# Attention and two expert layers on one core: a second PSUM bank for the sums of products with v, one bank fewer for the products of the maxima, no pause between heads

## The chip, the cores and the metric

The kernel runs on one core of one Trainium2 chip. The metric is the device time of one execution in microseconds; the time of a kernel is the median of its runs. Five engines work side by side on a core: TensorE (PE, with its weight loads shown as PEld), VectorE (DVE), ScalarE (ACT), GpSimd (POOL) and SyncE (SP), which here issues loads and stores (DMA). Each works through its own instructions in order and waits on semaphores for what others produce. TensorE writes its results into PSUM, a memory in banks, and VectorE and ScalarE read them there.

## What is computed

An attention in which each query sees only the keys of its own cluster, then a mixture of experts with one expert for each token, then a dense layer. Cut to what matters:

```python
# B, H, S, D = 2, 8, 768, 64; 16 clusters
q_assign = argmax(einsum('bhsd,hcd->bhsc', q_n, c_n)); k_assign likewise
mask = q_assign[:, :, :, None] == k_assign[:, :, None, :]
scores = where(mask, (q @ k.T) / sqrt(D), -1e9)
attn = exp(scores - scores.max(-1)); attn /= attn.sum(-1) + 1e-9
x = (attn @ v)                       # -> 1536 tokens x 512
e = argmax(x @ w_gate + modality_bias[modality_id])       # 8 experts
x = gate[e] * (relu(x @ w1[e]) @ w2[e])                   # 512 -> 1024 -> 512
h = x @ w_in                                              # 512 -> 2048
out = (h * tanh(softplus(h))) @ w_out                     # 2048 -> 512
```

## The kernel before

There are 16 heads (2 batches of 8), numbered i, and each head has six blocks of 128 keys, numbered kt. `attention()` is a generator that walks over n = 6 i + kt. For each n it does, in program order:

- `st_step`: four matmuls (L391) that give the transposed scores of one block of keys against all 768 queries, in two tiles of one PSUM bank each (`s` from pool `ps_s`, or `eps` from `ps_e`), and two exponentials on ScalarE (L393). ScalarE then rounds the result to f16 (`eh`, L400) and GpSimd forms the remainder (`el`, a subtraction in L114); for kt 2 and 5 it is used in f32 as it is (`ef`).
- `smax`: the row maxima of a head one to two ahead. Matmuls of the masked products (L350 with 512 columns; L355 twice 256 columns) write a tile `x` of pool `ps_x`, one bank each, nine for a head. VectorE reduces each tile to maxima (L351, L356) and, after the six blocks, to `mx` (L363). ScalarE makes `m16` of it (L366), six transposes (`mrow_b`, L373) write one more tile `x`, and ScalarE copies it into the operand of the next head (L378). So the scores of a head wait for the maxima of that head.
- `av_step`: the sums of products with v, three blocks behind (LAG = 3). For each block 18 matmuls (L427, L428, L429 with `eh` and `el`) or 6 in f32 (L425) add into the head's tile `av` of pool `ps_a`, which takes one bank for the whole head. `fin` reads it when the head is done: VectorE forms r from the sums (L440, L441) and xt (L442), ScalarE and GpSimd write the two halves of x.

`assign` finds the clusters of a head three ahead: 24 small matmuls (L273), a chain on VectorE (L286, L287, L289, L290, L292, L299) and GpSimd, a copy on ScalarE, and four DMAs that write the result into the head's operand `QK` (L303). `stack` loads the operand of a head three ahead with four DMAs (L258 to L261). At the start of head 1, `gate_consts` loads the constants of the gate with three DMAs, and twelve slots later VectorE prepares them (L683 to L693).

Pieces like `fin`, `assign` and `gate_consts` lie in a list `side`, from which `slot()` takes one or two at each of three places in a step. `avq` holds the blocks whose sums are due, and `av_next` takes one or two of them at two places in a step. It also holds a pause: when the head before is finished it sets `gap[0] = GAP`, and at the first block of the next head it returns so many times without work, so that the sums of the new head, which need the one bank of `ps_a`, are issued a step later.

The order in which instructions then stand on PE, DVE, ACT and POOL is not the program order: a scheduler lays all instructions out on a modelled time line, in which each PSUM bank is free again after its last reader, and fixes the order of each engine from it. SyncE keeps the program order. So another number of banks moves instructions on several engines all through attention.

After batch 0 is gated (`gate`), expert matmuls (L1027, `moe1`) and the conversion of w_in (`convs`, L1047 to L1055) are mixed into the heads of batch 1. When attention is over its pools are closed, four banks go to the last part (L1027 into `h`, L1183 into `o`), and the rest of the experts runs beside it.

Eight banks are held by four pools while attention runs: `ps_e` 2 (tag `e`), `ps_s` 2, `ps_x` 3, `ps_a` 1.

Of the kernel before, what the change touches and what calls it, by code (L numbers as in the profile page):

```python
# [16 lines left out]
PSUM = bass.MemoryType.PSUM  # L17
# [7 lines left out]
def clustered_attention_moe_kernel(  # L25
# [32 lines left out]
    LOWD = ()  # L58
    LOWE = ()
    PREG = 12  # L60
    GAP = 1
    AVL = 1
    ASK = 2
    CV1 = 20
# [29 lines left out]
    att = ExitStack()  # L94
# [5 lines left out]
    dp = ctx.enter_context(tc.tile_pool(name="dp", bufs=1, space=DRAM))  # L100
    ps_e = ctx.enter_context(tc.tile_pool(name="ps_e", bufs=2, space=PSUM))
    ps_s = att.enter_context(tc.tile_pool(name="ps_s", bufs=2, space=PSUM, side="right"))
    ps_x = att.enter_context(tc.tile_pool(name="ps_x", bufs=3, space=PSUM, side="right"))
    ps_a = att.enter_context(tc.tile_pool(name="ps_a", bufs=1, space=PSUM, side="right"))
    ap = att.enter_context(tc.tile_pool(name="ap", bufs=1, side="right"))
    a2 = att.enter_context(tc.tile_pool(name="a2", bufs=2, side="right"))
    a3 = att.enter_context(tc.tile_pool(name="a3", bufs=3, side="right"))
# [386 lines left out]
    def attention():  # L494
# [41 lines left out]
        def av_next():  # L536

            k = 1 + (len(avq) > AVL)
            while avq and k:
# [9 lines left out]
                if j == 1 and kt == T - 1:  # L549
                    gap[0] = GAP  # L550
                    if i % H == H - 1 and FAST:
# [840 lines left out]
```

## Time and profile before

| | us |
|---|---|
| three runs, median | 678.7 (677.6 to 678.86) |
| the profiled execution | 680.72 |
| its span in the profile | 679.0 |
| PE busy | 620.5 (91%) |
| ACT busy | 454.6 (67%) |
| DVE busy | 378.3 (56%) |
| POOL busy | 255.4 (38%) |

The table gives averages over a span with different parts. Attention reaches to about 312 us; behind it stand the experts and the dense layers. A matmul's row ends with a modelled drain, and matmuls overlap, so rows of PE that follow each other closely start more often than their lengths suggest, and a PE that is "busy" is not at its peak. An engine's wait is told in the views by the instruction that ended it ("<- DVE xt L442": the wait ended when VectorE's L442 had written xt). PEclk is the clock that TensorE was granted, as a share of its full speed.

### The profile page before, as it was taken

The page shows a single profiled execution, that of the slowest core. Times are in us where ns is not written, and L with a number is a line of the kernel's source. Part 1 is how long each engine was busy: PE and PEld are TensorE (multiplying, and loading weights), DVE is VectorE, ACT ScalarE, POOL GpSimd, SP SyncE. Part 2 cuts the span into 40 slices and gives each one's busy share as a digit, 9 for nine tenths or more (in the row PEclk, how much of TensorE's full clock was granted, in tenths as well). Part 3 has the DMA queues.
Part 4 walks back from the last instruction along what each step waited for, and adds up shares of the span by engine and source line. Part 5 has one row for each costly group of instructions (what it writes and reads, how often), then busy time and mean ns, then how long its engine had stood idle before and what let it go on. Part 6 is the DMA issues. An engine that isn't in the chain of part 4 may idle for free. (4 is left out here: it accounts for less than half of the span.)

```text
span 679.0 us, 13674 instructions
## 1 busy us (share of the span) xinstructions
PE 620.5 (91%) x5474; PEld 424.5 (63%) x5475; DVE 378.3 (56%) x747; ACT 454.6 (67%) x704; POOL 255.4 (38%) x226
## 2 busy tenths in 40 slices
PE   1798989989788998998999899999999999999995
PEld 1476768858466765665766567566666667666442
DVE  5776667687879899989658899622311101101000
ACT  4686787977787777655888686665655576767300
POOL 5464875886865344320521221111311222223111
PEclk9797999999899999999999999999999999999998
DMA  7542343412872353473455555211000000000000
GB/s 230 150 85 54 89 140 104 110 42 61 257 221 75 107 155 94 141 206 120 143 152 204 156 156 178 70 49 46 32 1 1 16 17 0 32 1 16 17 32 35
DMA packets 56742, 64.42 MB, mean 95 GB/s; under 512 B 10080, under 2 KB 46944, under 8 KB 56672
## 3 DMA queue, kind: packets, MB, share of 16 engines
q1 hardware_dynamic: 42064, 48.74, 25.3%
q10 hardware_dynamic: 12688, 8.42, 4.1%
q0 software_dynamic: 1920, 6.32, 2.6%
q8 instruction: 45, 0.74, 0.5%
q14 instruction: 25, 0.20, 0.1%
HBM read 46.23 MB, written 6.32 MB: 77 GB/s over the span
## 5 line engine op out<-in xcount | busy, mean ns | idle before, releaser
L114 POOL TENSOR_TENSOR el<-e,eh 128x768 f16<-128x768 f32 x64 | 108.0, 1691 | 84.9 <-ACT eh L400 52.1
L1027 PE MATMUL h<-x,win 128*128 128x256 f16 x1152 | 131.8, 273 | 0.2 <-POOL x L1014 0.2
L1027 PEld LDWEIGHTS <-win 128*128 128x128 f16 x1152 | 112.6, 98 | 19.0 <-issue 0.4
L1027 PEld LDWEIGHTS <-w 128*128 128x128 f16 x768 | 74.4, 98 | 66.8 <-issue 11.1
L1132 DVE SCALAR_TENSOR_TENSOR s<-s,h 128x512 f32<-128x512 f32 x48 | 30.8, 684 | 148.9 <-ACT s L1128 148.9
L1183 PE MATMUL o<-wout,xb 128*128 128x512 f16 x432 | 95.9, 379 | 0.0
L114 POOL TENSOR_TENSOR xb<-s,xb 128x1024 f16<-128x1024 f32 x18 | 40.2, 2231 | 134.0 <-ACT xb L1135 134.0
L391 PE MATMUL s<-QK 128*128 128x384 f16 x320 | 78.6, 335 | 5.8 <-issue 2.1
L1027 PE MATMUL eps<-xw,w 128*128 128x416 f16 x384 | 72.8, 339 | 8.2 <-DVE hT L989 2.9
L1027 PE MATMUL eps<-hT,w 128*128 128x416 f16 x384 | 71.8, 339 | 1.6 <-DVE hT L989 1.6
L351 DVE TENSOR_REDUCE mxh<-x 128x1 f32<-128x512 f32 x96 | 64.7, 681 | 14.6 <-PE x L350 14.2
L1183 PEld LDWEIGHTS <-xb 128*128 128x128 f16 x432 | 42.2, 98 | 48.3
L393 ACT ACTIVATE e<-s 128x384 f32<-128x384 f32 x112 | 52.5, 489 | 23.1 <-PE s L391 19.1
L400 ACT ACTIVATE eh<-e 128x768 f16<-128x768 f32 x64 | 54.1, 847 | 0.8
L425 PE MATMUL av<-vst,ef 128*128 128x65 f32 x384 | 51.1, 276 | 0.0
L425 PEld LDWEIGHTS av<-vst,ef 128*128 128x128 f32 x384 | 49.8, 196 | 1.9
L427 PE MATMUL av<-vst,eh 128*128 128x65 f16 x384 | 46.0, 195 | 5.2 <-DVE xt L442 4.7
L391 PEld LDWEIGHTS <-QK 128*128 128x128 f16 x384 | 34.6, 103 | 22.1 <-issue 10.0
L1126 ACT ACTIVATE s<-h,cst 128x512 f32<-128x512 f32 x48 | 32.9, 685 | 21.7 <-PE h L1027 21.5
L428 PE MATMUL av<-vst,eh 128*128 128x64 f16 x384 | 46.2, 196 | 0.0
L350 PE MATMUL x<-QK 128*128 128x512 f16 x96 | 37.9, 404 | 8.6 <-DMA QK<-oT 5.1
L942 DVE SCALAR_TENSOR_TENSOR w<-wf,w 128x1024 f16<-128x1024 f32 x32 | 43.4, 1357 | 3.9 <-ACT w L938 3.9
(244 smaller groups left out, 1100.9 us busy)
## 6 DMA issues: line engine op xcount, KB each, us to landing
wf<-in_moe_w_dram ACTq DMA_DIRECT2D x16, 512.0 KB
raw<-in_moe_w_in_dram SPq DMA_DIRECT2D x16, 512.0 KB
raw<-in_moe_w_out_dram SPq DMA_DIRECT2D x16, 512.0 KB
wf<-in_moe_w_dram SPq DMA_DIRECT2D x16, 512.0 KB
QK<-hl SPq DMA_DIRECT2D x32, 192.0 KB
xs<-dr SPq DMA_DIRECT2D x12, 258.0 KB
t<-in_k_dram SPq DMA_DIRECT2D x8, 384.0 KB
t<-in_q_dram SPq DMA_DIRECT2D x8, 384.0 KB
```

The source lines that it names most:

```text
L114: nc.gpsimd.tensor_tensor(out=out_, in0=in0, in1=in1, op=ALU.subtract)
L350: nc.tensor.matmul(sp, lhsT=st[:, QA, t * P:(t + 1) * P], rhs=st[:, KA, 0:512], start=True, stop=True)
L351: nc.vector.reduce_max(out=mx_t[i][:, t, 0:1], in_=sp, axis=AX.X)
L391: nc.tensor.matmul(sps[hf][:, 0:HS], lhsT=st[:, KA + a, kt * P:(kt + 1) * P], rhs=st[:, QA + a, hf * HS:(hf + 1) * HS], start=(a == 0), st ...
L393: nc.scalar.activation(out=e32[:, hf * HS:(hf + 1) * HS], in_=sps[hf][:, 0:HS], func=AF.Exp, scale=1.0 / float(D) ** 0.5)
L400: nc.scalar.activation(out=eh, in_=e32, func=AF.Copy)
L425: nc.tensor.matmul(av[:, t, :], lhsT=e32[:, cols], rhs=vs[:, h, :], start=(kt == 0 and t == 0), stop=(kt == T - 1), skip_group_check=True)
L427: nc.tensor.matmul(av[:, t, :], lhsT=eh[:, cols], rhs=vs[:, h, 0:NV], start=(kt == 0 and t == 0), stop=False, skip_group_check=True)
L428: nc.tensor.matmul(av[:, t, 0:D], lhsT=eh[:, cols], rhs=vs[:, h, NV:], start=False, stop=False, skip_group_check=True)
L942: nc.vector.scalar_tensor_tensor(out=hl_[:, 1], in0=f, scalar=32.0, in1=hl_[:, 0], op0=ALU.mult, op1=ALU.subtract)
L1027: nc.tensor.matmul(out_, lhsT=wc[:, a, kk, ms], rhs=mv[:, c, kk, :], start=(i == 0), stop=(i == n - 1))
L1183: nc.tensor.matmul(pts[t], lhsT=gsl[q % 2][f // FB][:, f % FB, a, t * P:(t + 1) * P], rhs=wout[:, c, f, :], start=(f == 0 and i_ == 0), st ...
```

## The change

Three numbers change. `ps_x`, the pool of the tiles of maxima, gets two banks instead of three; `ps_a`, the pool of the sums, gets two instead of one, so that the sums of one head can begin while `fin` of the head before still reads its own; GAP, the pause of `av_next` at a new head, is 0. The banks in use remain eight. No instruction is added or removed.

```diff
@@ -58,7 +58,7 @@
     LOWD = ()
     LOWE = ()
     PREG = 12
-    GAP = 1
+    GAP = 0
     AVL = 1
     ASK = 2
     CV1 = 20
@@ -100,8 +100,8 @@
     dp = ctx.enter_context(tc.tile_pool(name="dp", bufs=1, space=DRAM))
     ps_e = ctx.enter_context(tc.tile_pool(name="ps_e", bufs=2, space=PSUM))
     ps_s = att.enter_context(tc.tile_pool(name="ps_s", bufs=2, space=PSUM, side="right"))
-    ps_x = att.enter_context(tc.tile_pool(name="ps_x", bufs=3, space=PSUM, side="right"))
-    ps_a = att.enter_context(tc.tile_pool(name="ps_a", bufs=1, space=PSUM, side="right"))
+    ps_x = att.enter_context(tc.tile_pool(name="ps_x", bufs=2, space=PSUM, side="right"))
+    ps_a = att.enter_context(tc.tile_pool(name="ps_a", bufs=2, space=PSUM, side="right"))
     ap = att.enter_context(tc.tile_pool(name="ap", bufs=1, side="right"))
     a2 = att.enter_context(tc.tile_pool(name="a2", bufs=2, side="right"))
     a3 = att.enter_context(tc.tile_pool(name="a3", bufs=3, side="right"))
```

What the change does to the order shows best at three places. In these rows a number behind a name tells tiles of one name apart.

The first place is the turn from head 0 to head 1 on PE. `av_541` are the sums of head 0, `av_806` (before) and `av_803` (after) those of head 1; x_748 belongs to the maxima of head 2, x_844 to those of head 3; s_836, eps_835 and s_766 are scores of head 1. Before:

```order
L350 MATMUL x_844<-QK3_120 128x512
L391 LDWEIGHTS QK1_118
L391 MATMUL s_836<-QK1_118 128x384
L391 LDWEIGHTS QK1_118
L391 MATMUL s_836<-QK1_118 128x384
L427 LDWEIGHTS eh_650
L427 MATMUL av_806<-vst_293,eh_650 128x65
L428 LDWEIGHTS eh_650
L428 MATMUL av_806<-vst_293,eh_650 128x64
```

and after:

```order
L391 MATMUL eps_835<-QK1_118 128x384
L427 LDWEIGHTS eh_650
L427 MATMUL av_803<-vst_293,eh_650 128x65
L428 LDWEIGHTS eh_650
L428 MATMUL av_803<-vst_293,eh_650 128x64
L350 LDWEIGHTS QK2_119
L350 MATMUL x_748<-QK2_119 128x512
L391 LDWEIGHTS QK1_118
L391 MATMUL s_766<-QK1_118 128x384
```

The first two sums of head 1 now stand ahead of x_748, x_774 and x_813, which stood ahead of them before (as x_803 did in place of x_813), and the rest of its first block behind x_774.

The second place is the same turn on DVE: mxh_588 collects the maxima of head 2, L683 to L693 prepare the constants of the gate (idf from the DMA's idr, wg from wgf), L440 and L442 read the sums of head 0. Before:

```order
L356 TENSOR_REDUCE mxh_588<-x_630 128x2
L351 TENSOR_REDUCE mxh_588<-x_639 128x1
L299 STREAM_TRANSPOSE oC_690<-so2_556 128x384
L351 TENSOR_REDUCE mxh_588<-x_660 128x1
L356 TENSOR_REDUCE mxh_588<-x_705 128x2
L683 CAST idf_665<-idr_663 128x12
L351 TENSOR_REDUCE mxh_588<-x_723 128x1
L351 TENSOR_REDUCE mxh_588<-x_748 128x1
L686 TENSOR_SCALAR em_886<-idf_665 128x12
L692 TENSOR_SCALAR wg_133<-wgf_668 128x4x8
L688 TENSOR_TENSOR biasT_132<-mb_666,em_886 128x96
L693 SCALAR_TENSOR_TENSOR wg_133<-wgf_668,wg_133 128x4x8
```

and after:

```order
L356 TENSOR_REDUCE mxh_588<-x_630 128x2
L683 CAST idf_665<-idr_663 128x12
L686 TENSOR_SCALAR em_886<-idf_665 128x12
L688 TENSOR_TENSOR biasT_132<-mb_666,em_886 128x96
L686 TENSOR_SCALAR em_889<-idf_665 128x12
L688 TENSOR_TENSOR bt_891<-mb_666,em_889 128x96
L351 TENSOR_REDUCE mxh_588<-x_639 128x1
L692 TENSOR_SCALAR wg_133<-wgf_668 128x4x8
L690 TENSOR_TENSOR biasT_132<-biasT_132,bt_891 128x96
L693 SCALAR_TENSOR_TENSOR wg_133<-wgf_668,wg_133 128x4x8
L440 TENSOR_SCALAR r_758<-av_541 128x6
L351 TENSOR_REDUCE mxh_588<-x_660 128x1
```

L683 and four small operations moved ahead of the reduction of x_639, L692 and L693 ahead of that of x_660. Behind these rows, before, came L440, and after it the reduction of x_774, L441 and L442; after the change come L441, the reduction of x_705, L442, the reductions of x_723, x_748 and x_774.

The third place is the start on DVE: mxh_315 collects the maxima of head 0, and L363 makes mx_364 of them; eps_368 are the similarities of head 2 for `assign`. Before:

```order
L286 TENSOR_REDUCE smx_393<-eps_368 128x12
L351 TENSOR_REDUCE mxh_315<-x_347 128x1
L287 TENSOR_TENSOR eps_368<-eps_368,smx_393 128x192
L356 TENSOR_REDUCE mxh_315<-x_352 128x2
L351 TENSOR_REDUCE mxh_315<-x_361 128x1
L289 TENSOR_TENSOR eps_368<-eps_368,desc_105 128x192
L363 TENSOR_REDUCE mx_364<-mxh_315 128x6
L290 TENSOR_REDUCE smx_393<-eps_368 128x12
L292 TENSOR_TENSOR seq_394<-eps_368,smx_393 128x192
```

and after:

```order
L356 TENSOR_REDUCE mxh_315<-x_338 128x2
L289 TENSOR_TENSOR eps_368<-eps_368,desc_105 128x192
L351 TENSOR_REDUCE mxh_315<-x_344 128x1
L290 TENSOR_REDUCE smx_393<-eps_368 128x12
L351 TENSOR_REDUCE mxh_315<-x_347 128x1
L292 TENSOR_TENSOR seq_394<-eps_368,smx_393 128x192
L356 TENSOR_REDUCE mxh_315<-x_352 128x2
L351 TENSOR_REDUCE mxh_315<-x_361 128x1
L363 TENSOR_REDUCE mx_364<-mxh_315 128x6
```

L290 and L292 moved from behind L363 to places ahead of it.

On SP the order is the same in both kernels, but for the numbers of tiles.

## Rows read from the trace of the kernel before

**Rows 1.** Stretches: busy us of PE, PEld, DVE, ACT, POOL; PEclk, DMA share, GB/s.

```profile
36.00:165.00 129.00, 120.61 (x1551) 94.70 (x1550) 91.97 (x205) 101.19 (x196) 89.17 (x81) 0.96 0.36 90
165.00:200.00 35.00, 28.52 (x359) 22.07 (x357) 28.10 (x83) 27.55 (x54) 26.86 (x24) 0.95 0.74 220
200.00:312.00 112.00, 101.28 (x1048) 70.11 (x1046) 102.77 (x170) 78.04 (x145) 43.39 (x30) 1.00 0.44 128
312.00:671.00 359.00, 352.16 (x2367) 226.60 (x2365) 132.13 (x234) 225.81 (x277) 75.79 (x49) 1.00 0.21 66
```

**Rows 2.** Waits of DVE, 200 to 312 us: total us, times, longest.

```profile
DVE mxh L351 <- PE x L350: 0.2, 1, 0.2
```

**Rows 3.** Waits of PE, 36 to 165 us.

```profile
PE av L427 <- DVE xt L442: 3.2, 2, 2.1
...
PE x L350 <- DVE mxh L351: 0.5, 1, 0.5
```

**Rows 4.** Waits of PE, 165 to 320 us.

```profile
PE av L427 <- DVE xt L442: 1.5, 2, 0.8
PE x L350 <- DVE mxh L351: 1.2, 2, 0.9
PE x L350 <- DVE mxh L356: 1.1, 1, 1.1
...
PE x L355 <- DVE mxh L356: 0.6, 1, 0.6
```

**Rows 5.** Order of time on DVE, 42 to 53 us: start, us, instruction [idle before <- releaser].

```profile
42.24 0.69 DVE L356 TENSOR_REDUCE mxh<-x 128x2 f32<-128x512 f32 x1 [1.53 <-PE x L355]
...
45.97 0.17 DVE L683 CAST idf<-idr 128x12 f32<-128x12 int32 x1 [0.50 <-DMA idr<-in_moe_modality_id_dram]
...
47.50 1.62 DVE L692 TENSOR_SCALAR wg<-wgf 128x32 f16<-128x32 f32 x1
...
49.20 1.63 DVE L693 SCALAR_TENSOR_TENSOR wg<-wgf,wg 128x32 f16<-128x32 f32 x1
...
51.13 0.16 DVE L440 TENSOR_SCALAR r<-av 128x6 f32<-128x6 f32 x1
...
52.24 0.56 DVE L442 TENSOR_TENSOR xt<-av,r 128x384 f32<-128x384 f32 x1
```

**Rows 6.** Order of time on PE, 44 to 53 us.

```profile
44.78 0.59 PE L350 MATMUL x<-QK 128*128 128x512 f16 x2
...
46.99 0.78 PE L425 MATMUL av<-vst,ef 128*128 128x65 f32 x6
...
50.29 0.49 PE L391 MATMUL s<-QK 128*128 128x384 f16 x2
52.85 0.20 PE L427 MATMUL av<-vst,eh 128*128 128x65 f16 x1 [2.08 <-DVE xt L442]
```

**Rows 7.** Order of time on SP's queue, 36 to 56 us.

```profile
40.46 0.51 SPq L258 DMA_DIRECT2D QK<-hl  x1
...
43.05 0.59 SPq L676 DMA_DIRECT2D idr<-in_moe_modality_id_dram  x1
```

**Rows 8.** The stretch 54 to 62 us, columns as in rows 1.

```profile
54.00:62.00 8.00, 8.00 (x58) 5.82 (x55) 3.37 (x8) 3.65 (x9) 4.29 (x5) 0.57 0.33 73
```

**Rows 9.** Tile x: count, duration in ns (least/median/most), first and last start in us.

```profile
L350 PE MATMUL x<-QK x96: 376/379/634, 19.4 to 260.0; 128*128 128x512 f16 x96
...
L351 DVE TENSOR_REDUCE mxh<-x x96: 645/681/693, 20.3 to 263.3; 128x1 f32<-128x512 f32 x96
```

**Rows 10.** Order of time on DVE, 26 to 29 us.

```profile
27.48 0.16 DVE L363 TENSOR_REDUCE mx<-mxh 128x6 f32<-128x12 f32 x1
27.60 0.36 DVE L290 TENSOR_REDUCE smx<-eps 128x12 f32<-128x192 f32 x1
```

**Rows 11.** Order of time on PE, 24 to 37 us.

```profile
27.93 0.80 PE L373 MATMUL x<-ident,m 128*2 128x128 f16 x6 [2.53 <-ACT m L366]
```

**Rows 12.** Order of time on PE, 306 to 320 us.

```profile
310.15 4.38 PE L1027 MATMUL eps<-xw,w 128*128 128x416 f16 x24
```

## Prediction

> **What bounds the kernel now.** I read the stretches first, then what each engine waited for in them, then the order of time at single places, then the tiles. The span is 679.0 us and the profiled execution 680.72, so 1.7 us lie around the span; that execution is 2.0 us above the median of the runs, 678.7. The sum below is a difference, made against the profiled execution and then put on the median.
>
> From 312 us on TensorE is busy for 352.2 of 359 us [rows 1]. Attention is over there and its PSUM pools are closed, so the change can only move the moment at which that part begins, and how much MoE work is done by then. Attention has three stretches. From 36 to 165 us (heads 0 to 7) TensorE is busy 120.6 of 129 us, with ScalarE at 101, VectorE at 92 and GpSimd at 89: no other engine is nearly full, so a stop of TensorE here is mostly lost. From 165 to 200 us the gate of batch 0 and its weights come in (DMA share 0.74), and TensorE idles 6.5 us. From 200 to 312 us VectorE is busy 102.8 of 112 us [rows 1] and waits only 0.2 us for a tile of maxima [rows 2]: there VectorE sets the end, and a wait of TensorE costs little.
>
> **What the single bank of sums costs today.** A head's sums (`av`) stay in their bank until VectorE has read them in L440 and L442. TensorE waited for that 3.2 us in two turns between heads before 165 us [rows 3], and 1.5 us in two after it [rows 4]. The largest, 2.08 us, is the turn from head 0 to head 1: the last sum of head 0 is finished at 47.77, but L440 comes only at 51.13, because VectorE is in the two slow operations on the gate weights, L692 (1.62 us) and L693 (1.63 us). TensorE goes on at 52.85 [rows 5, 6]. The other 11 of the 15 turns show no such wait: the pause of a step (GAP) and the order put other matmuls there.
>
> **Part 1: a second bank for the sums.** The turn no longer waits for L442. Of the 3.2 us, 2.08 belong to the first turn, which I treat by itself below, since the order changes there on both engines. The other 1.1 us go: **-1.1**, between 0 and -1.1. The 1.5 us after 165 us I cost at nothing, as VectorE's 102.8 busy us cover most of that time; if that cover is gone they are worth -1.5. GAP=0 adds and removes no instruction; it lets the sums of a head start a step earlier in program order.
>
> The Trainium skill (Perfetto Trace Analysis, "Optimizing Tensor Performance", Matmuls) says that independent matmul groups should rotate through different PSUM banks, so that emptying one overlaps the next. Taken for the sums alone it would give back 3.2 + 1.5 us, 674.0 us; but the same sentence holds for the maxima, which lose a bank, and 11 turns without a wait show that an order can hide a single bank too.
>
> **Part 2: two banks for the maxima.** In the trace the third bank was in use when a tile was written (both tiles before it still unread) for 23 of the 91 tiles begun from 36 to 165 us, 11.7 us of lead in all, and for 6 of 20 from 165 to 200 us, 7.5 us. These are worked out from the start of each tile's first matmul and the end of its reduction, 0.68 us long [rows 9]. With two banks such a matmul must come later or wait. The new order moves most of them: on VectorE 42 of the 143 successive reductions stand directly behind each other, against 63. Tight places remain: tiles with fewer than ten matmuls on TensorE since the last one into the same bank are 7 (2 before) for heads 0 to 7, and 2 (0 before) in the middle stretch. What they cost is not in the trace; the nearest rows are the waits for a bank of maxima, 0.5 us once before 165 us [rows 3], and 2.9 us in four waits after it [rows 4]. For heads 0 to 7, one wait of 0.5 for two tight places gives 1.2 for five more; I take **+1.0**, since one of the five lies in the first turn (ends: 0, and the whole lead, 11.7). In the middle two more at 0.7 each, 2.9 over 4: **+1.4** (ends 0 and 7.5). After 200 us VectorE covers it.
>
> **Part 3: the turn from head 0 to head 1.** VectorE works in order, and its order changes there. Before, the casts and products of the gate constants stand behind the reductions of x_639, x_660 and x_705. Now L683, which needs a DMA, stands ahead of x_639, and L692 and L693 ahead of x_660. The data of L683 are there at 45.97 [rows 5]: SyncE issues the load at 43.05, behind the four loads of the next head, which begin at 40.46 [rows 7]. SyncE's order is the same in both kernels, and what frees those loads, the last scores of head 0, has its place on TensorE about as before. So, with durations from [rows 5]:
> - x_630 is read by 42.93 (42.24 + 0.69). VectorE then stands until 45.97 for L683; before, it read three tiles first and then waited 0.5.
> - L683 (0.17) and four small operations of about 0.2, as L440 has, take 1.0, the reduction of x_639 0.7: 47.7 us. x_705 needs that bank.
> - L692, L690 (small, 0.2), L693, L440 and the reduction of x_660 (1.62, 0.2, 1.63, 0.16, 0.69) take 4.3: 52.0 us. x_723 needs that bank; before, it was written at 44.78 [rows 6].
> - L441 (0.2), the reduction of x_705, L442 and the reduction of x_723 (0.69, 0.56, 0.69) end at 54.1, and x_774 needs that bank.
>
> TensorE by then lacks two tiles of maxima and a pair of scores that it had done at 52.85. Two tiles are 0.59 us, a pair of scores 0.49 [rows 6], with ends that overlap: 0.7 in all. So the turn ends 54.1 - 52.85 = 1.3 later and 0.7 behind in work: **+2.0**. The ends are -2.1, if nothing waits, and +5.3, if two stops of 2.6 and 2.7 us at x_705 and x_723 displace nothing.
>
> **The clock.** After the 2.08 us wait the granted clock is 0.57 in the mean from 54 to 62 us, for most of that time the lower of its two levels, 1.2 of 2.4 GHz [rows 8]. At the higher one the same work would have taken 8 x (1 - 0.57) = 3.4 us less. Since a stop remains in this turn, I cost it at **0**; ends -3.4 (no stop, no fall) and +3.4 (a second fall).
>
> **The start.** Ahead of head 0's scores TensorE waits 2.53 us for the row maxima [rows 11], which hang on L363 on VectorE at 27.48. In the new order L290 and L292 of the next assignment stand ahead of L363, where before they stood behind it. L290 takes 0.36 us [rows 10], and L292 is of the same size: **+0.7**, ends 0 and +1.2 (if VectorE also waits for the similarity matmuls, which now stand nearly in one piece ahead of x_338).
>
> **MoE work done early.** Ahead of the first matmul of the last part (`h`) stand 276 expert matmuls instead of 264. Twelve more are 2.2 us (24 take 4.38 [rows 12]). From 200 to 312 us TensorE has 10.7 us idle for them [rows 1]: I take half, **-1.1**, ends -2.2 and 0.
>
> **Sum**: -1.1 + 1.0 + 1.4 + 2.0 + 0 + 0.7 - 1.1 = +2.9. The profiled execution would be 683.6, the median **681.6**.
>
> **Rivals.**
> *The wait goes and nothing takes its place* (faster). Mechanism: L683's data land before VectorE comes to it, so x_705 and x_723 find their banks free. The turn then gives -2.1 in place of +2.0, and half the clock's loss, -1.7: 681.6 - 4.1 - 1.7 = 675.8. It decides at the landing: by 43 us, not 45.97. For it: the sums of head 1 do stand earlier in the order. Against it: the four loads ahead on SyncE. If the clock comes back whole and the other terms take their best ends, 678.7 - 3.2 - 1.5 - 3.4 - 2.2 = 668.4.
>
> *One wait for another* (no change): tiles of maxima come to cost what the sums cost, 4.7 us in all, and the rest cancels: 678.7. For it: behind both waits stands the same VectorE. The Trainium skill (TensorE: Matmul & The Clock Gate, "HAM oscillation") reports a kernel in which double buffering in PSUM gave no further gain, 126.6 us against 125.5. By that this change would end here too; no row so far shows it.
>
> *Two banks tie the engines together* (much slower): half the lead that the third bank gave is lost on TensorE, 5.9 + 3.8 in place of 1.0 + 1.4: 681.6 + 7.3 = 688.9. Against it: the order leaves a median of 26 matmuls between two uses of a bank for heads 0 to 7 (35 before).
>
> *The change does not do what it says*: the sums of the next head might not come earlier. The order shows that they do: the first two of head 1 stand ahead of three tiles of maxima that belong to head 2.
>
> **How the numbers follow.** Forecast 0.42, one wait for another 0.18, the wait gone 0.30, much slower 0.10. 0.2% is 1.4 us, about what a measurement of this kernel can tell from no change: faster is below 677.3, slower above 680.1. A little of the forecast's chance falls between: faster 0.30, same 0.19, slower 0.51. The range goes from 672.5, which leaves out the better part of the faster case, to 688.0, short of the slowest case; the forecast's own is 679.5 to 686.
>
> **What would show it.** Right: VectorE idle ahead of L683 for 2 to 3 us; TensorE waiting at L355 or L350 for a reduction between 45 and 54 us, 2 to 5 us in all; no wait of L427 for L442; waits of L350 and L355 for L351 and L356 of 6 us or more in the whole trace; the last part beginning 2 to 5 us later. Wrong: L683 without a wait, a granted clock of 1.00 from 54 to 62 us, or a last part of another length than now.

## The result, and the profile after the change

The changed kernel takes 687.0 us in the median of 4 runs (684.6 to 691.8), the kernel before 678.8 on the same chip: a ratio of 1.0121, with a 95% interval of 1.008 to 1.0163. Run again with the first experiments it took 685.3 us in the median of 10 runs (683.0 to 691.3), a ratio of 1.0078 (1.0053 to 1.0104). So it is slower by 5 to 8 us. The forecast was 681.6 in a range up to 688.0: the direction was right, the size too small, and most of the loss came from another place than the one forecast.

The profiled execution of the changed kernel is the longest of its four, 691.8 us with a span of 690.2. Its stretches, columns as in [rows 1] (the third ends and the last begins 4 us later than there, as attention lasts longer):

```profile
36.00:165.00 129.00, 120.98 (x1554) 93.12 (x1554) 89.64 (x198) 103.03 (x198) 90.52 (x81) 0.99 0.35 89
165.00:200.00 35.00, 24.61 (x272) 17.23 (x272) 29.94 (x78) 21.59 (x39) 23.96 (x22) 0.76 0.67 199
200.00:316.00 116.00, 106.63 (x1123) 76.67 (x1120) 97.96 (x166) 79.41 (x155) 44.22 (x30) 0.97 0.42 120
316.00:684.00 368.00, 357.47 (x2406) 229.84 (x2405) 142.68 (x251) 231.04 (x285) 78.77 (x51) 1.00 0.21 69
```

Against [rows 1] the first stretch looks the same: TensorE is busy 121.0 us of 129 (120.6 before). The second does not: TensorE is busy 24.6 of 35 us, not 28.5, and its clock is 0.76, not 0.95. In the third VectorE is no longer nearly full: it idles 18.0 of 116 us (9.2 of 112 before).

The waits of TensorE for tiles of maxima and sums, first from 36 to 165 us, then from 165 to 320 us, where [rows 3, 4] stood:

```profile
PE x L355 <- DVE mxh L351: 2.2, 2, 1.4
PE x L350 <- DVE mxh L351: 2.1, 2, 1.3
...
PE x L350 <- DVE mxh L356: 0.4, 1, 0.4
```

```profile
PE x L350 <- DVE mxh L351: 6.2, 1, 6.2
PE x L350 <- DVE mxh L356: 3.7, 2, 3.1
PE s L391 <- ACT w L938: 3.6, 1, 3.6
PE x L355 <- DVE mxh L351: 3.0, 3, 2.6
```

The wait of L427 for L442 is gone: 4.7 us in four turns before, none after. Waits of L350 and L355 for a reduction are 4.7 us in the first stretch (0.5 before) and 12.9 us in the second (2.9 before). One of them is 6.2 us long, the longest wait of TensorE in attention. VectorE's order of time shows what it stood behind:

```profile
184.00 0.16 DVE L836 CAST nblk<-gab 128x8 int32<-128x8 f32 x1
184.07 0.19 DVE L441 RECIPROCAL r<-r 128x6 f32<-128x6 f32 x1
184.26 8.16 DVE L942 SCALAR_TENSOR_TENSOR w<-wf,w 128x1024 f16<-128x1024 f32 x1
192.34 0.34 DVE L286 TENSOR_REDUCE smx<-eps 128x12 f32<-128x192 f32 x1
192.61 0.67 DVE L351 TENSOR_REDUCE mxh<-x 128x1 f32<-128x512 f32 x1
```

L942 prepares expert weights and takes 1.2 us elsewhere (its line stands twice more within 15 us of this one, at 1.23 and 1.22). Here it takes 8.16. GpSimd at that time, and TensorE behind the reduction that stood in line after L942:

```profile
184.90 1.66 POOL L114 TENSOR_TENSOR el<-e,eh 128x768 f16<-128x768 f32 x1
186.50 3.23 POOL L249 TENSOR_TENSOR hl<-t,hl 128x768 f16<-128x768 f32 x2
189.69 1.63 POOL L114 TENSOR_TENSOR el<-e,eh 128x768 f16<-128x768 f32 x1
```

```profile
193.33 0.59 PE L350 MATMUL x<-QK 128*128 128x512 f16 x1 [6.23 <-DVE mxh L351]
```

GpSimd ran four operations without a gap until 191.3. L942 ended 1.1 us after that, about its own length. TensorE had filled both banks of maxima and stood 6.2 us. Its clock was 0.50 from 181 to 197 us. The clock fell ahead of this wait, around another stop, in which the scores waited behind ScalarE's L938 for a load of expert weights:

```profile
181.92 0.80 PE L391 MATMUL s<-QK 128*128 128x384 f16 x2 [3.55 <-ACT w L938]
```

The kernels with three banks have a stop at this place too, of 2.1 to 4.0 us, so it is not of the change.

The first turn went as forecast in its place. VectorE (first fence) waits at L683 with the reductions behind it, and TensorE (second fence) stops twice for a bank:

```profile
50.25 0.17 DVE L683 CAST idf<-idr 128x12 f32<-128x12 int32 x1 [2.12 <-DMA idr<-in_moe_modality_id_dram]
...
52.16 1.63 DVE L692 TENSOR_SCALAR wg<-wgf 128x32 f16<-128x32 f32 x1
...
53.87 0.18 DVE L693 SCALAR_TENSOR_TENSOR wg<-wgf,wg 128x32 f16<-128x32 f32 x1
```

```profile
52.29 0.38 PE L355 MATMUL x<-QK 128*128 128x256 f16 x2 [1.36 <-DVE mxh L351]
...
54.77 0.58 PE L350 MATMUL x<-QK 128*128 128x512 f16 x1 [0.84 <-DVE mxh L351]
```

### The profile page after: what moved, and what is told of

The parts are those of the page before. It is cut to its first block, busy times and chain, and to the rows that moved or that the text cites. A ratio compares the mean times of both kernels' runs of the same rounds, so it can differ in the third digit from the quotient of the medians.

```text
span 690.2 us, 13663 instructions
## 1 busy us (share of the span) xinstructions
PE 625.8 (91%) x5474; PEld 425.6 (62%) x5475; DVE 382.4 (55%) x747; ACT 454.3 (66%) x704; POOL 255.7 (37%) x226
## 5 line engine op out<-in xcount | busy, mean ns | idle before, releaser
L391 PE MATMUL s<-QK 128*128 128x384 f16 x320 | 80.6, 345 | 5.7 <-ACT w L938 3.6
L1027 PE MATMUL eps<-xw,w 128*128 128x416 f16 x384 | 74.7, 341 | 5.9 <-DVE hT L989 3.7
L350 PE MATMUL x<-QK 128*128 128x512 f16 x96 | 40.3, 423 | 16.0 <-DVE mxh L351 8.6
L942 DVE SCALAR_TENSOR_TENSOR w<-wf,w 128x1024 f16<-128x1024 f32 x32 | 50.6, 1580 | 5.6 <-ACT w L938 5.2
L428 PE MATMUL av<-vst,eh 128*128 128x64 f16 x384 | 50.8, 196 | 0.0
L427 PE MATMUL av<-vst,eh 128*128 128x65 f16 x384 | 50.5, 195 | 0.2 <-ACT eh L400 0.2
L425 PEld LDWEIGHTS av<-vst,ef 128*128 128x128 f32 x384 | 48.3, 194 | 1.3
```

What stands on the lines that cost most here:

```text
L350: nc.tensor.matmul(sp, lhsT=st[:, QA, t * P:(t + 1) * P], rhs=st[:, KA, 0:512], start=True, stop=True)
L391: nc.tensor.matmul(sps[hf][:, 0:HS], lhsT=st[:, KA + a, kt * P:(kt + 1) * P], rhs=st[:, QA + a, hf * HS:(hf + 1) * HS], start=(a == 0), st ...
L425: nc.tensor.matmul(av[:, t, :], lhsT=e32[:, cols], rhs=vs[:, h, :], start=(kt == 0 and t == 0), stop=(kt == T - 1), skip_group_check=True)
L427: nc.tensor.matmul(av[:, t, :], lhsT=eh[:, cols], rhs=vs[:, h, 0:NV], start=(kt == 0 and t == 0), stop=False, skip_group_check=True)
L428: nc.tensor.matmul(av[:, t, 0:D], lhsT=eh[:, cols], rhs=vs[:, h, NV:], start=False, stop=False, skip_group_check=True)
L942: nc.vector.scalar_tensor_tensor(out=hl_[:, 1], in0=f, scalar=32.0, in1=hl_[:, 0], op0=ALU.mult, op1=ALU.subtract)
```

## The experiments

The spans below are read by the moment at which `xt` of a head (L442) is done, since each head passes through it; "head 8 to 10" is the time from `xt` of head 8 to that of head 10. The kernel before was run beside each group; its medians were 679.8, 680.5 and 680.0 us.

### The three parts of the change, one and two at a time

The changed kernel, run again without an edit:

> The changed kernel once more, unaltered. It tells how much its time and its trace differ from execution to execution: the four runs so far lie between 684.6 and 691.8 us, and in the profiled one VectorE's L942 at 184 us took 8.16 us, while GpSimd ran four operations one behind the other; in the trace of before the longest took 2.58. Theory (the long L942 is a matter of where it falls against GpSimd's work, so it differs between executions): the time is 684 to 688 us and the longest L942 is clearly shorter or longer than 8 us. Rival (it lies in the order of the instructions and is there each time): again near 8 us, and the time 685 to 692.

Measured: 685.3 us, ratio 1.0078 (1.0053 to 1.0104). The long L942 did not come again: at its place L942 took 1.18 us and the one after it 2.22. It began 0.70 us ahead of GpSimd's first subtraction (0.64 in the first profile) and this time was not held up; the subtraction took 1.97 us instead of 1.64, and a small operation that followed (0.15 us elsewhere) ended as the subtraction did:

```profile
187.83 1.18 DVE L942 SCALAR_TENSOR_TENSOR w<-wf,w 128x1024 f16<-128x1024 f32 x1
...
189.79 0.74 DVE L837 TENSOR_SCALAR nblk<-nblk 128x8 int32<-128x8 int32 x1
```

```profile
188.53 1.97 POOL L114 TENSOR_TENSOR el<-e,eh 128x768 f16<-128x768 f32 x1
```

One bank of maxima taken away, and nothing given for it:

```diff
-    ps_x = ... bufs=3
+    ps_x = ... bufs=2
```

> Of the three numbers only the bank of the maxima is taken away (two banks there, one for the sums, a pause of one step; seven banks in use). Theory (the bank of the maxima is what costs, and the second bank of the sums gives back a few us): slower than the changed kernel or like it, 687 to 692 us, with 8 us or more of TensorE's waits for a reduction of maxima, and again waits for L442 of 3 us or more. Rival (the second bank of the sums, or the missing pause, is what costs): near the kernel before, 677 to 681.

Measured: 694.0 us, ratio 1.0208 (1.0164 to 1.0252), more than was expected; the waits for L442 were 1.7 us from 36 to 320 us, not 3 or more.

The banks of the change, with the pause left in (GAP = 1):

> Both pools as in the changed kernel, with the pause of a step left in (GAP=1). Theory (the pause matters little once there are two banks): within 2 us of the changed kernel, 684 to 689 us. Rival (the sums that start early push maxima and scores back, and that is the cost): 677 to 681 us.

Measured: 689.8 us, ratio 1.014 (1.0093 to 1.0187). That is 4.5 us above the changed kernel run again, not within 2, so the expectation missed.

The banks as before, without the pause (GAP = 0):

> The banks of the kernel before, with the pause alone taken out (GAP=0). Theory (the pause only places the wait for the bank of the sums): 678 to 682 us, with TensorE's waits for L442 at 4.7 us or a few more. Rival (the missing pause is what costs): 684 us or more.

Measured: 679.9 us, ratio 1.0006 (0.9975 to 1.0036).

The bank of maxima is what costs: 14 us by itself. The second bank of sums gives about 4 of them back and the missing pause some 3 to 4 more (694.0, 689.8, 685 to 687). These two steps are less sure than the first: the losses lie at 11 to 17, 6 to 13 and 4 to 7 us by their intervals, which overlap from one to the next. With three banks of maxima the pause is worth nothing (0.4 us, from -1.7 to 2.4). The waits of TensorE for a bank of maxima from 36 to 320 us part the kernels with two from those with three: 17.7 us in the changed kernel, 13.9 and 14.9 in the two others with two banks, against 1.5 in the last run of this group and 3.4 before the change. Among the kernels with two banks they do not rank the times.

### The loads of w_in

In batch 1 VectorE waits for pieces of w_in with a reduction behind them, and TensorE then for the bank. Here in the changed kernel:

```profile
253.49 0.43 DVE L1047 TENSOR_SCALAR f<-raw 128x512 int32<-128x512 int32 x1 [3.24 <-DMA raw<-in_moe_w_in_dram]
...
255.29 0.68 DVE L356 TENSOR_REDUCE mxh<-x 128x2 f32<-128x512 f32 x1
```

```profile
256.02 0.58 PE L350 MATMUL x<-QK 128*128 128x512 f16 x1 [3.08 <-DVE mxh L356]
```

So fourteen of the sixteen loads of w_in were left out, in both kernels; their conversions read the first two pieces again:

```diff
-            if nm == "i":
+            if nm == "i" and j >= RAWB:
+                raw_t[nm, j] = first[j % RAWB]
+            elif nm == "i":
                 conv_load(...)
+                first[j] = raw_t[nm, j]
```

> The changed kernel, but of the 16 pieces of w_in only the first two are loaded; the other 14 conversions read these two again (so the last part computes with wrong weights; the work on VectorE, ScalarE and TensorE is the same). The load is taken out of VectorE's way: in the changed kernel VectorE waited 4.9 us at L1047 for such a load from 200 to 330 us (2.7 before the change), once for 3.24 us with a reduction (L356) queued behind, for whose bank TensorE then waited 3.08 us. Theory 'a wait of VectorE now reaches TensorE, since two banks of maxima give no lead': the waits at L1047 go and with them most of those 3 us and part of the rest: 681 to 683.5 against the 685.3 of the changed kernel run again. Rival 'two banks cost the same whatever VectorE waits for, by the order alone': 684.5 to 686, the waits of L350 and L355 still 15 us or more in all.

Measured: 685.7 us, ratio 1.0072 (1.0049 to 1.0096). The theory falls. VectorE's waits at L1047 went from 4.9 to 0.8 us, and nothing was gained. The waits of TensorE from 165 to 320 us in this run:

```profile
PE x L355 <- DVE mxh L351: 4.0, 3, 2.6
...
PE x L350 <- DVE mxh L356: 3.0, 2, 2.8
PE x L350 <- DVE mxh L351: 1.8, 2, 1.2
```

They still hold 8.8 us for banks of maxima (13.6 from 36 us on, where the rival said 15 or more). The edit also moved the order: 252 expert matmuls stand ahead of the last part, not 276, so this run alone does not prove that the waits are those of the order.

> The same edit (14 of 16 loads of w_in left out, their conversions read the first two pieces) in the kernel before. Theory 'three banks give the lead that hides VectorE's waits': the 2.7 us that VectorE waited at L1047 from 200 to 330 us go, and the time moves by less than 1.5 us: 678.3 to 680. Rival 'these loads hold up either kernel': 2 us or more below 679.8, and then the gain of the other run says nothing of the banks.

Measured: 680.0 us, ratio 1.0003 (0.9983 to 1.0023). The loads hold up neither kernel.

### The gate's constants, loaded earlier

```diff
+                if n == 5:
+                    put(start(gate_consts(), 1), 12)
                 if kt == 0:
                     if i + 3 < NH:
                         stack(i + 3)
-                    if i == 1:
-                        put(gate_consts())
```

> The changed kernel with the three loads of the gate's constants issued at the last block of head 0 instead of at the start of head 1, so that on SyncE they stand ahead of the four loads of head 4's operand; VectorE's L683 to L693 then stand among the reductions of head 1's end and not behind x_630. The prediction's term for this turn, +2.0 (VectorE's wait of 2 to 3 us at L683 with a reduction and two tiles of maxima behind it): 683.3 against 685.3. From the trace after the change, in which head 1 ends only 1.1 us later than before: the turn is worth 0.5 or less, 684.8. Rival 'L683's wait has no part in it': 685.3 within 0.7, with TensorE's waits of 45 to 55 us (3.3 to 4 us in the runs so far) still there at other instructions.

Measured: 684.0 us, ratio 1.0061 (1.0038 to 1.0085). L683 still waits 1.04 us for its load, at 40.85 us, but from 44 to 56 us TensorE waits 0.2 us for a bank of maxima (2.2 in the changed kernel). The gain of 1.3 us is smaller than the intervals can tell from none.

> The same edit in the kernel before. There TensorE waited 2.08 us at the turn from head 0 to head 1 for the reading of the sums, behind the two products on the gate's weights (1.62 and 1.63 us), and its granted clock was 0.57 from 54 to 62 us. If that stop and the low clock behind it cost what the prediction put as ends (2.1 and up to 3.4 us): 674.5 to 677.7, faster than the kernel before. If TensorE makes up for it, as head 1 of the changed kernel made up for 2.0 of 3.1 us: 678.5 to 679.8. Rival 'the new order costs elsewhere': above 680.5.

Measured: 680.1 us, ratio 0.9997 (0.9975 to 1.0019). The stop of 2.08 us in the first turn [rows 3, 6] was gone, and the stretch in which the clock had been 0.57 [rows 8] was at full clock:

```profile
54.00:62.00 8.00, 8.00 (x119) 6.72 (x117) 4.34 (x10) 5.32 (x12) 5.67 (x7) 1.00 0.48 123
```

Head 1 was done at 67.0 us (68.0 before), but head 8 at 165.9 (165.2). So in this pair of executions what the stop and the low clock had cost in the first turn was made up for by 165 us, and this kernel is no better than the one before. The stop alone does not set the clock of that stretch: two more kernels with three banks there have it, 2.07 us (no pause alone) and 2.08 us (two banks from head 10 on), and were at 1.00.

### Two banks in one part of attention only

The pools were closed and opened again at one step, with the other numbers of banks (`banks` opens `ps_x` and the second bank of sums; the pause goes with them). Until the switch shows (at 61 to 62 us or at 174 to 176 us), TensorE's order is that of the kernel before, or of the changed one, row for row.

```diff
+            if n == T * SW:
+                banks(1)
             i, kt = divmod(n, T)
```

> Banks as in the changed kernel (two for the maxima, two for the sums, no pause) up to the scores of head 10, then as in the kernel before (three, one, a pause); the order of all engines is that of the changed kernel up to about 160 us. Prediction's view (its terms up to 200 us +4.0, after that nothing): still +2 to +4 of the loss here, 682 to 684 if the kernel before takes 680. View from the traces since ('batch 1 loses 3 to 4 us in every execution by waits for maxima, the start and the first turn lose the rest'): 681.5 to 683, and xt of head 15 within 2 us of where xt of head 10 would put it in the kernel before (103.7 to 105 us later). Rival 'all loss is at the start and the first turn': 685 or more.

Measured: 685.3 us, ratio 1.0094 (1.0065 to 1.0124).

> The reverse: banks as before up to the scores of head 10, then as in the changed kernel; the order is that of the kernel before up to about 160 us. Prediction's view ('after 200 us VectorE covers it', the middle stretch +1.4, MoE work done early -1.1): within 1 us of the kernel before, 679.5 to 681. View from the traces: 3 to 4 us slower, 683 to 684.5, with 5 us or more of waits of L350 and L355 for reductions from 200 us on (1.2 in the kernel before).

Measured: 681.9 us, ratio 1.0036 (1.002 to 1.0052).

> Banks as in the changed kernel only up to the scores of head 2 (the order is that of the changed kernel up to about 60 us), then as before: the start and the turn from head 0 to head 1 alone. Prediction's view: +0.7 and +2.0, less 1.1 for nothing: 682 to 683 against 680. View from the traces (xt of head 0 2.5 us later, of which 2.0 come back in head 1; more in executions whose clock falls): +0.5 to +2.5, 680.5 to 682.5. Rival 'the turn's delay is made up for altogether': within 0.5 us of before.

Measured: 679.6 us, ratio 0.9989 (0.9959 to 1.0018).

> The reverse: as before up to the scores of head 2, then as in the changed kernel: everything but the start and the first turn. If the parts add up, its loss and that of the run with two banks up to head 2 make the whole of the changed kernel (5 to 7 us): 683 to 685. If heads 2 to 9 cost nothing by two banks, it is as the run that goes to two banks at head 10, within 1 us.

Measured: 688.8 us, ratio 1.0118 (1.0086 to 1.015).

None of the four came out as the views before it said. The late part costs 2.4 us, more than the prediction's view and less than the 3 to 4 of the other. The start with the first turn costs nothing (-0.7 us, with an interval from -2.8 to +1.2), as its rival said. Two banks up to head 10 cost more than either view (685.3 us; head 15 came 108.4 us after head 10, not 103.7 to 105), and two banks from head 2 on more than the 683 to 685 expected (688.8). The loss lies between: heads 2 to 9 make 6.4 + 0.7 = 7.1 us by the first and third of these runs, or 8.0 - 2.4 = 5.6 by the fourth and second. In single profiled executions it is less. In the mean of five with three banks (the kernel before, no pause alone, without loads, constants earlier, two from head 10) `xt` of heads 2, 8 and 10 is done at 81.3, 165.2 and 203.0 us; in five of the changed kernel and its nearest variants (twice unaltered, without loads, constants earlier, two until head 10) at 81.2, 166.8 and 206.5. So nothing is lost by head 2, 1.6 us by head 8, 3.5 by head 10.

In the two kernels that lose there, the long VectorE instruction stands again, at another operation (lines of these kernels are 15 to 18 higher: L854 is L836). First the run with two banks up to head 10, then the run with two banks from head 2:

```profile
181.15 6.77 DVE L854 CAST nblk<-gab 128x8 int32<-128x8 f32 x1
```

```profile
183.61 7.83 DVE L854 CAST nblk<-gab 128x8 int32<-128x8 f32 x1
```

A cast of eight numbers in a row, 0.16 us in the changed kernel, took 7.83. GpSimd in that last run:

```profile
184.11 3.26 POOL L129 TENSOR_TENSOR el<-e,eh 128x768 f16<-128x768 f32 x2
187.33 0.90 POOL L462 TENSOR_TENSOR xb<-xt,xb 128x384 f16<-128x384 f32 x1
188.20 3.22 POOL L264 TENSOR_TENSOR hl<-t,hl 128x768 f16<-128x768 f32 x2
```

The cast ends at 191.44, GpSimd's series at 191.42. TensorE waited 6.3 and 6.0 us for a bank of maxima in these two runs, and its clock from 180 to 200 us was 0.64 and 0.66. The second of them:

```profile
180.00:200.00 20.00, 12.60 (x107) 8.82 (x107) 17.63 (x20) 11.82 (x21) 12.18 (x12) 0.66 0.77 237
```

Put together, over all profiled executions of the study but the run with two banks up to head 2, first the way to head 8 and then the gate's stretch. The clock is that of 54 to 62 us:

| banks of maxima, heads 2 to 9 | clock | `xt` of head 8 done, us |
|---|---|---|
| three | 0.57; 0.79; 1.00 (three executions) | 165.2; 166.0; 164.2 to 165.9 |
| two | 0.57 | 171.2 |
| two | 0.79 to 0.80 (three) | 166.6 to 168.4 |
| two | 1.00 (four) | 164.6 to 167.4 |

| banks of maxima, heads 2 to 9 | VectorE instruction of 6.8 to 9.0 us near 184 us | head 8 to head 10, us |
|---|---|---|
| two (changed, one bank fewer alone, two until head 10, two from head 2) | yes | 42.5, 45.3, 41.9, 43.8 |
| two (changed again, no loads, constants earlier, pause left in) | no | 37.5, 39.3, 37.2, 39.0 |
| three (five executions) | no | 37.1 to 38.9 |

Two things stand out in these heads. The first is that a delay is not made up for. With three banks `xt` of head 2 is done at 79.7 to 82.7 us and that of head 8 at 164.2 to 166.0, so a spread of 3.0 us shrinks to 1.9. In the five with two banks just named it is 79.1 to 85.3 and 164.6 to 171.2: all of it stays. A low clock in the first turn is one source of delay, not the only one. The changed kernel was 1.7 us behind the run without loads at head 0, with a clock of 1.00 until then, and 3.0 at head 8; the same program run again was 3.1 behind at head 0, after a clock of 0.53 from 24 to 42 us, and 6.5 at head 8. The second is the long instruction, worth 43.4 - 38.3 = 5.1 us where it comes. Where neither comes, two banks cost little up to head 10: it was done at 204.0 and 202.9 us in the runs without loads and with earlier constants, against 201.7 to 203.7 with three banks (206.4 with the pause left in). The long instruction stood in one profile of the changed kernel and not in the next, with the same program, so it hangs on timing. None in five with three banks and four in eight with two is too few to prove that two banks make it likelier. The order speaks for it, though. With three banks the cast and the second L942 are through 0.1 to 4.6 us before GpSimd's series begins; with two, one of them begins 0.3 to 0.7 us ahead of the series in all eight executions. Four were then held up (0.3, 0.5, 0.6, 0.6) and four not (0.3, 0.3, 0.7, 0.7), so what decides between them is not shown.

## Why the prediction was right, and where it was not

**Direction and mechanism.** The time fell into the range with some luck: of the terms, the largest (+2.0, the first turn) measured nothing, and the heads forecast at +1.3 made most of the loss. That tiles of maxima would cost more than the sums had cost was right. The waits for L442 went, as Part 1 said, and waits for reductions took their place (17.7 us for 4.7 + 3.4).

**Part 1** was right on its wait (4.7 us to none). The experiments add what it did not see: with two banks of maxima the second bank of sums and the missing pause matter more, some 4 us each by the medians, than with three, where the pause alone gives nothing.

**Part 2, heads 2 to 9**, is the step that failed. With Part 1 it came to -1.1 + 1.0 + 1.4 = +1.3; the runs give 5.6 to 7.1. Up to 165 us the waits for banks of maxima rose by 4.2 us, not 1.0, but other waits went and TensorE was as busy as before. The loss shows in delays that are not made up for by head 8, and in the middle stretch. The +1.4 of that stretch was two waits of 0.7 us, taken from rows of three-bank waits; the wait that came was 6.2 us. The working took every VectorE operation at its usual length. The trace of before had a sign that lengths are not fixed. In it L942 took 2.58 us in one place, while GpSimd was in its series (from 182.45 to 191.43 us, in these rows):

```profile
182.45 3.30 POOL L114 TENSOR_TENSOR el<-e,eh 128x768 f16<-128x768 f32 x2 [1.00 <-ACT eh L400]
185.72 3.24 POOL L249 TENSOR_TENSOR hl<-t,hl 128x768 f16<-128x768 f32 x2
188.93 0.91 POOL L447 TENSOR_TENSOR xb<-xt,xb 128x384 f16<-128x384 f32 x1
189.80 1.63 POOL L114 TENSOR_TENSOR el<-e,eh 128x768 f16<-128x768 f32 x1
```

```profile
189.94 2.58 DVE L942 SCALAR_TENSOR_TENSOR w<-wf,w 128x1024 f16<-128x1024 f32 x1 [1.33 <-ACT w L938]
```

The series stands in both kernels. Before, the two L942 ahead of it are through by 182.4 and the next comes near its end; after the change an L942 comes 0.6 us ahead of where it begins. The Trainium skill (SBUF — State Buffer, "SBUF: two separate sides") says that VectorE and GpSimd share a port pair, which one holds for a whole instruction while the other is blocked. The trace agrees that VectorE is blocked until GpSimd is through, in four executions for the rest of a series of four or five instructions and not for one. In the same program run again it was let in between two of them: L837 ended at 190.53, the first subtraction at 190.50, the series ran on.

**After 200 us**, "VectorE covers it" fell. VectorE was busy 102.8 of 112 us before and hardly waited for tiles of maxima (0.2 us, [rows 2]); with two banks it waits for them 3.2 us and idles 18 us in all. TensorE waited 6.5 us for banks of maxima there in the changed kernel. From head 10 to GpSimd's last instruction four executions of the changed order took 3.4 us more than six with three banks there (473.0 to 474.6 against 470.0 to 471.3); the run that changes only this part gave 2.4 in its median. It is not a price of two banks in every order: the profiled executions with two banks from head 10 on and from head 2 on took 471.7 and 471.0. What makes up the loss was not settled: in the former the waits for banks of maxima after 205 us are only 1.4 us, and the loads of w_in are not the cause.

**Part 3** had the place, the instruction and the waits: VectorE idle for 2.12 us ahead of L683, TensorE stopped for 1.36 + 0.84 us. As a term of the sum its +2.0 was wrong. L693 took 0.18 us, not the 1.63 of [rows 5], and the delay did not last: two banks in the start and the first turn alone cost nothing. What a stop there costs in the end seems to hang on the heads behind it, which the sum took as they were; no run changed those heads alone with the stop in place.

**The clock** was costed at nothing, with ends of 3.4 us either way, and here the ends were the better guide. From 54 to 62 us it was 0.79 in the changed kernel, 0.57 in the same program run again and 1.00 in the run without loads, whose order is the same up to there. From head 0 to head 1, across that stretch, the first two lost 1.3 and 2.8 us against the third, which is near 8 x (1 - 0.79) = 1.7 and 8 x (1 - 0.57) = 3.4; none of it had come back at head 8 (167.7, 171.2 and 164.7 us). The stretch in the same program run again:

```profile
54.00:62.00 8.00, 6.82 (x60) 4.44 (x60) 6.11 (x19) 3.72 (x7) 2.52 (x3) 0.57 0.14 48
```

In the kernel before, one execution without the stop had no low clock there and the time stayed as it was; but two with the stop had none either. So the start and the first turn became a place where executions of one program part by some 6 us, 3 of them by head 0.

**The start** was too small: L363 came at 29.05, not 27.48 [rows 10], 1.6 us later for the 0.7 forecast and 1.2 at most. Besides L290 and L292, TensorE now stops for banks ahead of it:

```profile
25.88 0.58 PE L350 MATMUL x<-QK 128*128 128x512 f16 x1 [0.57 <-DVE mxh L356]
26.75 0.59 PE L355 MATMUL x<-QK 128*128 128x256 f16 x2 [0.28 <-DVE mxh L351]
27.61 0.58 PE L350 MATMUL x<-QK 128*128 128x512 f16 x1 [0.28 <-DVE mxh L351]
```

By itself this too was worth nothing, as the run with two banks up to head 2 shows.

**MoE work done early** was right: 276 matmuls stand ahead of the last part, and from its first `h` to GpSimd's last instruction it takes 351.4 us, not 353.7: 2.3 us less, the forecast's end and not the half of it that was put into the sum.

**The rivals.** "The wait goes and nothing takes its place" fell, as L683 did wait. "One wait for another" fell as well, 678.7 being outside the interval, and with it what hung on the Trainium skill's sentence on double buffering (TensorE: Matmul & The Clock Gate, "HAM oscillation"). "Two banks tie the engines together" gave 688.9, and the two measurements lie between the forecast and it. It had the right pair of engines and nearly the right size, but put 5.9 us of it into heads 0 to 7, where the profiled executions lost 1.6 in the mean by head 8. The last part began 13.4 us later in the profiled execution (first `h` at 332.6, not 319.2) and 5.2 later in the run with earlier constants; 2 to 5 had been named.

## What to carry to other kernels

A bank that an order hardly ever waits for can still be the slack that absorbs another engine's rare long instruction, so count what a bank hides at its worst moment and not at the average wait. Look in the trace for one operation with several lengths: the longest, read beside what the other engines did just then, is a cost that a new order can move into the path. To find where in a long program a change costs, apply it to one part of the program at a time; here four such runs moved the blame from the first turn to heads 2 to 9 and, for a smaller part, to those behind them.

## What the hardware showed that was not expected

VectorE instructions stretched to 6.77, 7.83, 8.16 and 8.99 us while GpSimd ran subtractions back to back: a cast of 128x8 that takes 0.16 us elsewhere, and L942 at 1.2 us. The cast ended within 0.1 us of the end of GpSimd's series, and L942 1.1 us after it. In four other executions L942 began as close ahead of the series (0.3 to 0.7 us) and took 1.18. Reductions out of PSUM kept to 0.64 to 0.69 us throughout. In the first turn L692 and L693 took 1.62 and 1.63 us in one execution [rows 5] and 1.63 and 0.18 in another.
